# Products without use beside a sink attention, and half of its normalising moved to ScalarE

## The chip, the cores and the metric

The kernel runs on one core of one Trainium2 chip. The metric is the device time of a whole execution in microseconds (us). A core has a matrix engine (TensorE, PE), a vector engine (VectorE, DVE), an engine for activation functions (ScalarE, ACT), GpSimd (POOL) and SyncE (SP), whose queue here issues all transfers (DMA). The engines run side by side, each through its own list in order, and wait for each other by semaphores.

## The reference

Three layers follow each other. The first is an attention with a window and sinks (2 sequences, 8 heads, 768 positions, 64 values per head), the second and third are feed-forward layers on 1536 tokens with a model width of 512 and an inner width of 2048.

```python
def _attn_ref(q, k, v, n_sink, window):          # n_sink = 4, window = 128
    scores = scale * np.matmul(q, k.transpose(0, 1, 3, 2))
    keep = is_sink | in_window                   # pos_k < n_sink, or 0 <= pos_q - pos_k < window
    scores = np.where(keep, scores, -1e9)
    a = np.exp(scores - np.max(scores, axis=-1, keepdims=True))
    a = a / (np.sum(a, axis=-1, keepdims=True) + 1e-09)
    return np.matmul(a, v)

def _moe_ref(x, w_in, w_out):
    h = x @ w_in
    g = np.where(h >= 1, h, np.where(h <= -1, 0.0, (h + 1) ** 2 / 4))
    return g @ w_out

def _moe2_ref(x, w_in, w_out):
    h = x @ w_in
    return (h * np.clip(h + 3.0, 0.0, 6.0) / 6.0) @ w_out
```

The weights come as 8-byte floats, and the kernel narrows them on the chip.

## The kernel before

The attention is cut into units of 128 queries of a pair of heads. A unit goes through several steps. `score` multiplies queries and keys of both heads (L322) into two PSUM banks; DVE adds the mask and finds the extreme of each row (L329); ACT takes the exponential and its sum (`expo`, L348); `normalise` adds a small constant, takes the reciprocal (L340, L341) and multiplies each of the two heads by it (L343). Three units later `turn` transposes the probabilities on PE (L385, L386) and copies them out of PSUM (L367); `sinks` does it for the few sink columns (L397). When all units of a pair are turned, `mix` multiplies them with the values (L422) and splits the result into a high and a low part (L143, L150).

The feed-forward runs in fp32r, each f32 operand split into a high and a low part and three products for one: `h_group` (L546) makes the inner activations of 128 inner columns, two engines apply the activation function and split it (L555 to L560, L143, L150), and `y_group` (L590) adds its share of the output two slots later. The 1536 tokens are taken in chunks of 512, 256, 256 and 512 for the first layer and 512 three times for the second. Weights are loaded (`load_w`, L173), narrowed by DVE and ACT (`narrow`, L185 to L197) and split (`high`, `low`).

Orders: PE and SP keep the order in which the program is written. A list `steps` holds the attention's steps in order; its first 47 (begin, 21 scores, 17 turns, 4 sinks, 4 mixes) run ahead of the feed-forward, one after the other, with the weights taken between them; later steps are spread over the slots of the feed-forward. DVE and ACT are ordered by the compiler's scheduler. A planner (`Balance`) keeps a sum of expected nanoseconds for ACT and DVE; where either engine can do a copy, `pick` gives it to the one with the smaller sum. `defer` puts a piece of work some steps later. PSUM holds two banks for scores (tag "a"), four for outputs of the feed-forward (tags "y0" to "y3", lent to the transposes before) and two for inner activations (tag "h").

Of the kernel before, what the change touches and what calls it, by code (L numbers as in the profile page):

```python
# [8 lines left out]
F32 = mybir.dt.float32  # L9
# [3 lines left out]
AF = mybir.ActivationFunctionType  # L13
# [3 lines left out]
P = 128  # L17
# [8 lines left out]
N = 512  # L26
# [10 lines left out]

AHEAD = 8
WO_LEAD = 2

SLACK = 6

# [33 lines left out]
def sink_attention_moe_moe_kernel(  # L76
# [14 lines left out]
    nc = tc.nc  # L91
    B, H, _, S = q.shape
# [10 lines left out]
    consts = ctx.enter_context(tc.tile_pool(name="consts", bufs=1))  # L103
# [7 lines left out]
    ps_h = ctx.enter_context(tc.tile_pool(name="ps_h", bufs=2, space=bass.MemoryType.PSUM))  # L111
# [11 lines left out]
    def defer(fn, slots=1):  # L123
        waiting.append((clock[0] + slots, fn))

    def tick():
        clock[0] += 1
        due = [w for w in waiting if w[0] <= clock[0]]
        for w in due:
            waiting.remove(w)  # L130
            w[1]()

    def flush():
        while waiting:
            tick()

    bal = Balance()
# [23 lines left out]
        return xparts[ci]  # L161

    half = consts.tile([P, 1], F32, name="half")
    ident = consts.tile([P, P], F32, name="ident")


# [32 lines left out]
    def take(m, which, fc):  # L199

        t = raw.pop((m, which, fc))
        if which == "i":
            hi = wpool.tile([P, DM], F32R, tag=f"wih{fc}", name=f"wih{m}_{fc}")
            lo = wpool.tile([P, DM], F32R, tag=f"wil{fc}", name=f"wil{m}_{fc}")
            wi[m, fc] = (hi.rearrange("p (k f) -> p k f", f=P), lo.rearrange("p (k f) -> p k f", f=P))
        else:
            w = wo_tile(m, fc)
            hi, lo = w[:, 0, :], w[:, 1, :]

        def split(src):  # L210
            high(hi, src, DM)
            defer(lambda: low(lo, src, hi, DM))
            if which == "o":
                defer(lambda: nc.sync.dma_start(out=f32(wo_d[m][fc]), in_=f32(w.rearrange("p a f -> p (a f)"))), 4)

        if wide:
            t32 = raw_p.tile([P, DM], F32, tag="w32", name="w32", bufs=3)
            narrow(t, t32)
            defer(lambda: split(t32), 2)
        else:  # L220
            split(t)
# [27 lines left out]
    def build_fast_attention(at_p):  # L249
        def key_column(i):  # L250
            return i * P + max(i - 1, 0) * NS
# [25 lines left out]
        def geom(gi):  # L277
            ci, b, i0, nq = GROUPS[gi]
            first = max(i0 - 1, 0)
            return b, i0, nq, first, i0 + nq - first  # L280

        def load(j):

            if j >= len(pairs):
                return
            gi, hp = pairs[j]
            b, i0, nq, first, nb = geom(gi)
            k0, k1 = key_column(first), key_column(i0 + nq - 1) + P
            r0 = 2 * hp * P + D
            tq = at_p.tile([P, NQ * P], F32, tag="qraw", name="qraw")[:, :nq * P]  # L290
            nc.sync.dma_start(out=tq, in_=q[b].rearrange("h r s -> (h r) s")[r0:r0 + P, i0 * P:(i0 + nq) * P])
            tk = at_p.tile([P, KW], F32, tag="kraw", name="kraw")[:, :k1 - k0]
            nc.sync.dma_start(out=tk, in_=k[b].rearrange("h r s -> (h r) s")[r0:r0 + P, k0:k1])
            qk[j] = (tq, tk)
# [17 lines left out]
        def score(j, u):  # L312
            b, i0, nq, first, nb = geom(pairs[j][0])
            tq, tk = qk[j]
            i = i0 + u
            w = widths[min(i, 2)]
            c0 = key_column(max(i - 1, 0)) - key_column(first)
            banks = []
            for e in range(2):
                rows = slice(e * D, (e + 1) * D)  # L320
                banks.append(ps_a.tile([P, 512], F32, tag="a", name="ps_s")[:, :w])
                nc.tensor.matmul(  # L322
                    banks[e], tq[rows, u * P:(u + 1) * P], tk[rows, c0:c0 + w], start=True, stop=True
                )
            p = at_p.tile([P, 2, KB + P], F32, tag="p", name="p", bufs=DIST + 3)[:, :, :w]
            nm = at_p.tile([P, 2], F32, tag="nm", name="nm", bufs=DIST + 2)
            sm = at_p.tile([P, 2], F32, tag="sm", name="sm", bufs=DIST + 2)
            for e in range(2):
                nc.vector.tensor_tensor_reduce(  # L329
                    out=p[:, e, :], in0=banks[e], in1=masks[min(i, 2)], scale=-SCALE, scalar=BIG,  # L330
                    op0=ALU.add, op1=ALU.min, accum_out=nm[:, e:e + 1],
                )
                bal.add("dve", 230 + w / 0.96)
            probs[j, u] = p
            if u == nq - 1:
                qk.pop(j)
                load(j + 2)

            def normalise():
                nc.vector.tensor_scalar_add(out=sm, in0=sm, scalar1=1e-9)  # L340
                nc.vector.reciprocal(out=sm, in_=sm)  # L341
                for e in range(2):
                    nc.vector.tensor_scalar_mul(out=p[:, e, :], in0=p[:, e, :], scalar1=sm[:, e:e + 1])  # L343
                bal.add("dve", 300 + 2 * (140 + w / 1.92))

            def expo():
                for e in range(2):
                    nc.scalar.activation(  # L348
                        out=p[:, e, :], in_=p[:, e, :], func=AF.Exp, scale=-1.0, bias=nm[:, e:e + 1],
                        accum_out=sm[:, e:e + 1],  # L350
                    )
                bal.add("act", 2 * (480 + w / 1.2))
                defer(normalise)

            defer(expo)
# [109 lines left out]
    def attend(upto):  # L465
        tick()
        first = True
        while done[0] < min(upto, len(steps)):
            if not first:
                tick()  # L470
            first = False
            steps[done[0]]()
            done[0] += 1
# [150 lines left out]
    def take_weights(s):  # L624
        while taken[0] < len(queue) and queue[taken[0]][0] <= s:
            take(*queue[taken[0]][1:])
            taken[0] += 1
            defer(load_weights, 4)

    x1_d = []  # L630
    with tc.manual_schedule(engines={mybir.EngineType.PE, mybir.EngineType.SP}):
        nc.vector.memset(half, 0.5)
        make_identity(nc, ident)
        with ExitStack() as att:
            if fast:
                at_p = att.enter_context(tc.tile_pool(name="at", bufs=2))
                build_fast_attention(at_p)
                attend(1)
                load_weights()
                n0 = ready[0]  # L640
                while done[0] < n0:
                    attend(done[0] + 1)
                    take_weights(-AHEAD + (AHEAD * done[0]) // n0 - 1)
            else:
                x1_d.append(dram.tile([DM, NT], F32, name="x1_d"))
                dense_attention(x1_d[0])
                load_weights()
                load_x1(0)
            take_weights(-1)
            flush()  # L650

            for s in range(len(seq) + LAG):
                lo = hi = fc = 0
                if s < len(seq):
                    ci, fc = seq[s]
                    m = chunks[ci][0]
                    if fast and ci + 1 < NCH:
                        lo, hi = ready[ci], ready[ci + 1]
                    if fc == 0:
                        flush()  # L660
                    if fc == 4 and ci + 1 < len(chunks):
                        if chunks[ci + 1][0]:
                            load_x(ci + 1)
                        elif not fast:
                            load_x1(ci + 1)
                sub = [0]

                def slot(fc=fc, lo=lo, hi=hi, sub=sub):
                    sub[0] += 1
                    total = 4 * FC - SLACK  # L670
                    attend(lo + (hi - lo) * min(4 * fc + sub[0], total) // total)

                a = s - LAG + WO_LEAD
                if 0 <= a < len(seq) and seq[a][0] not in (0, NCH):
                    load_wo(chunks[seq[a][0]][0], seq[a][1])
                if s < len(seq):
                    h_group(s, slot)
                    take_weights(s)
                    slot()
                if s >= LAG:  # L680
                    y_group(s - LAG, slot)
                slot()
            flush()
# [40 lines left out]
```

## Time and profile before

| | |
|---|---|
| time before, median of 3 runs | 681.76 us (679.98 to 683.12) |
| the profiled execution's own time | 683.12 us |
| its span, first to last instruction | 681.3 us |
| PE busy | 657.6 us (97%) |
| DVE busy | 415.9 us (61%) |
| ACT busy | 336.4 us (49%) |
| mean granted PE clock | 0.977 |

Busy time is the union of an engine's instructions. The granted clock is a share of full speed, 1.00 for 2.4 GHz and 0.50 for 1.2 GHz. PEld is the loading of weights into PE, which can overlap products. A wait is put down to what ended it.

### The profile page before, as it was taken

What the parts mean: (1) busy time and instruction counts of PE and PEld (TensorE: products, weight loads), DVE (VectorE), ACT (ScalarE), POOL (GpSimd) and SP (SyncE); (2) the same over time, 40 slices, a digit from 0 to 9 for tenths busy, and PEclk for the clock granted to TensorE, in tenths of its full rate; (3) what the DMA queues carried; (4) which work ended last, traced back from release to release, by engine and by line L of the source; (5) the groups of instructions that cost most, each with busy time, mean ns of one, the idle gap of its engine ahead of it and who ended that gap; (6) DMA issues with size and microseconds to landing.
All of it is one profiled execution on the core that took longest, in us unless ns stands there. A gap on an engine that the chain in (4) does not pass through costs nothing.

```text
span 681.3 us, 9471 instructions
## 1 busy us (share of the span) xinstructions
PE 657.6 (97%) x3392; PEld 523.7 (77%) x3392; DVE 415.9 (61%) x1031; ACT 336.4 (49%) x711; POOL 3.4 (0%) x19
## 2 busy tenths in 40 slices
PE   6988799999999999999999999999999999999997
PEld 3544567777788998888888887888888888888886
DVE  5978899998765556653779898598332222222222
ACT  5758776775454545553457575475222222322222
POOL 1000000000000000000000000000000000000000
PEclk9957899999999999999999999999999999999999
DMA  7234568656576446252398542994228222153321
GB/s 256 87 86 139 190 197 267 193 180 219 194 287 234 141 170 236 99 181 91 109 400 295 207 159 102 373 377 168 99 81 313 94 93 93 47 202 101 110 68 63
DMA packets 47023, 119.20 MB, mean 175 GB/s; under 512 B 4432, under 2 KB 15744, under 8 KB 46976
## 3 DMA queue, kind: packets, MB, share of 16 engines
q1 hardware_dynamic: 46976, 118.60, 49.9%
q8 instruction: 27, 0.44, 0.3%
q14 instruction: 20, 0.16, 0.1%
HBM read 92.36 MB, written 26.21 MB: 174 GB/s over the span
## 4 chain that ended last, share of the span: by engine, by line
PE 74%; DVE 11%; DMA 9%; ACT 3%; issue 1%; SPq 1%; ACTq 0%
PE ps_y L590 32%; PE ps_h L546 31%; DMA raw0i<-moe_w_in_dram 4%; PE ps_s L322 4%; PE ps_v L422 4%; DVE w L192 2%; DMA raw0o<-moe_w_out_dram 2%; DVE w L197 2%; DMA raw1o<-moe_w_out_dram 1%; PE ps_t L386 1%; DMA raw1i<-moe_w_in_dram 1%; PE ps_t L385 1%; ACT w L187 1%; PE ps_k L397 1%; DVE p L329 1%
## 5 line engine op out<-in xcount | busy, mean ns | idle before, releaser
L590 PE MATMUL ps_y<-gh,wo 128*128 128x512 f32 (+1 forms) x896 | 268.3, 364 | 1.6 <-ACT pt L367 1.3
L590 PEld LDWEIGHTS ps_y<-gh,wo 128*128 128x128 f32 x896 | 163.1, 189 | 31.5 <-issue 4.4
L546 PE MATMUL ps_h<-xh,wih 128*128 128x512 f32 (+1 forms) x448 | 165.9, 370 | 6.1 <-DVE gl L150 5.9
L546 PE MATMUL ps_h<-xl,wih 128*128 128x512 f32 (+1 forms) x448 | 161.5, 360 | 0.0
L546 PE MATMUL ps_h<-xh,wil 128*128 128x512 f32 (+1 forms) x448 | 161.5, 360 | 0.0
L590 PE MATMUL ps_y<-gl,wo 128*128 128x512 f32 (+1 forms) x448 | 160.9, 359 | 0.0
L150 DVE TENSOR_TENSOR gl<-ps_h,gh 128x512 fp32r<-128x512 f32 (+1 forms) x112 | 68.7, 613 | 87.4 <-ACT gh L143 87.3
L143 ACT ACTIVATE gh<-ps_h 128x512 fp32r<-128x512 f32 (+1 forms) x112 | 59.9, 535 | 110.4 <-PE ps_y L590 89.3
L546 PEld LDWEIGHTS ps_h<-xh,wih 128*128 128x128 f32 x448 | 84.7, 189 | 26.0 <-DVE gl L150 8.0
L546 PEld LDWEIGHTS ps_h<-xh,wil 128*128 128x128 f32 x448 | 84.8, 189 | 12.9
L546 PEld LDWEIGHTS ps_h<-xl,wih 128*128 128x128 f32 x448 | 84.9, 190 | 11.8
L590 PEld LDWEIGHTS ps_y<-gl,wo 128*128 128x128 f32 x448 | 84.6, 189 | 12.0
L560 DVE SCALAR_TENSOR_TENSOR ps_h<-r,ps_h 128x512 f32<-128x512 f32 x48 | 33.4, 696 | 85.3 <-ACT r L559 85.3
L559 ACT ACTIVATE r<-ps_h,half 128x512 f32<-128x512 f32 x48 | 33.0, 688 | 89.3 <-PE ps_h L546 89.3
L322 PE MATMUL ps_s<-kraw,qraw 64*128 64x260 f32 (+2 forms) x192 | 50.0, 495 | 11.4 <-DVE nm L329 6.9
L348 ACT ACTIVATE p<-p,nm 128x260 f32<-128x260 f32 (+2 forms) x96 | 46.5, 485 | 26.6 <-DVE nm L329 25.9
L329 DVE CUSTOM_DVE_ANT_0 p<-ps_s,mask 128x260 f32<-128x260 f32 (+2 forms) x96 | 36.8, 401 | 20.0 <-PE ps_s L322 19.8
L322 PEld LDWEIGHTS ps_s<-kraw,qraw 64*128 64x128 f32 x192 | 24.3, 228 | 27.9 <-DVE nm L329 14.8
L555 ACT ACTIVATE r<-ps_h,half 128x512 f32<-128x512 f32 (+1 forms) x64 | 36.7, 573 | 17.6 <-PE ps_h L546 17.1
L556 DVE SCALAR_TENSOR_TENSOR r<-r 128x512 f32<-128x512 f32 (+1 forms) x64 | 35.4, 554 | 15.5 <-ACT r L555 15.4
L190 DVE TENSOR_SCALAR w<-w 128x512 f32<-128x512 f32 x64 | 27.0, 422 | 17.1 <-ACT w L187 16.9
L557 DVE TENSOR_TENSOR ps_h<-ps_h,r 128x512 f32<-128x512 f32 (+1 forms) x64 | 35.9, 562 | 0.8
(59 smaller groups left out, 587.9 us busy)
## 6 DMA issues: line engine op xcount, KB each, us to landing
wo<-wo_d SPq DMA_DIRECT2D x80, 512.0 KB, 4.0
wo_d<-wo SPq DMA_DIRECT2D x32, 512.0 KB, 5.5
raw0i<-moe_w_in_dram SPq DMA_DIRECT2D x16, 512.0 KB, 4.7
raw0o<-moe_w_out_dram SPq DMA_DIRECT2D x16, 512.0 KB, 5.1
raw1i<-moe_w_in_dram SPq DMA_DIRECT2D x16, 512.0 KB, 5.4
raw1o<-moe_w_out_dram SPq DMA_DIRECT2D x16, 512.0 KB, 5.2
xh<-x2h_d SPq DMA_DIRECT2D x3, 1024.0 KB
xl<-x2l_d SPq DMA_DIRECT2D x3, 1024.0 KB, 9.5
```

The source lines that it names most:

```text
L143: nc.scalar.activation(out=dst, in_=src, func=AF.Copy)
L150: nc.vector.tensor_tensor(out=dst, in0=src, in1=f32(hi), op=ALU.subtract)
L322: nc.tensor.matmul(banks[e], tq[rows, u * P:(u + 1) * P], tk[rows, c0:c0 + w], start=True, stop=True)
L329: nc.vector.tensor_tensor_reduce(out=p[:, e, :], in0=banks[e], in1=masks[min(i, 2)], scale=-SCALE, scalar=BIG, op0=ALU.add, op1=ALU.min, a ...
L348: nc.scalar.activation(out=p[:, e, :], in_=p[:, e, :], func=AF.Exp, scale=-1.0, bias=nm[:, e:e + 1], accum_out=sm[:, e:e + 1],)
L546: nc.tensor.matmul(ps, w[:, kc, :], x[:, kc, :], start=i == 0, stop=i == len(ops) - 1)
L555: nc.scalar.activation(out=r, in_=ps, func=AF.Relu, scale=0.5, bias=half)
L556: nc.vector.scalar_tensor_tensor(out=r, in0=r, scalar=1.0, in1=r, op0=ALU.min, op1=ALU.mult)
L557: nc.vector.tensor_tensor(out=ps, in0=ps, in1=r, op=ALU.max)
L559: nc.scalar.activation(out=r, in_=ps, func=AF.Relu, scale=1.0 / 6.0, bias=half)
L560: nc.vector.scalar_tensor_tensor(out=ps, in0=r, scalar=1.0, in1=ps, op0=ALU.min, op1=ALU.mult)
L590: nc.tensor.matmul(ys[dm], a[:, cs], b, start=fc == 0 and i == 0, stop=fc == FC - 1 and i == 2)
```

## The change

`normalise` multiplies the first head on DVE as before; the second head is multiplied by ACT, as a copy with a scale per row, and the planner is told of it. A constant tile `warm` of 128x128 is filled with 0.5 by DVE. Ahead of the first chunk's feed-forward, eight products of `warm` with itself are issued on PE before the first score, and one after each of the following attention steps. They go to a tile of one of the two "h" banks, which nobody reads.

```diff
+WARM = 8
+WARM_STEP = 1
...
+    warm = consts.tile([P, P], F32, name="warm")
...
             def normalise():
                 nc.vector.tensor_scalar_add(out=sm, in0=sm, scalar1=1e-9)
                 nc.vector.reciprocal(out=sm, in_=sm)
-                for e in range(2):
-                    nc.vector.tensor_scalar_mul(out=p[:, e, :], in0=p[:, e, :], scalar1=sm[:, e:e + 1])
-                bal.add("dve", 300 + 2 * (140 + w / 1.92))
+                nc.vector.tensor_scalar_mul(out=p[:, 0, :], in0=p[:, 0, :], scalar1=sm[:, 0:1])
+                nc.scalar.activation(out=p[:, 1, :], in_=p[:, 1, :], func=AF.Copy, scale=sm[:, 1:2])
+                bal.add("dve", 300 + 140 + w / 1.92)
+                bal.add("act", 190 + w / 1.2)
...
+    def keep_warm(ps, n):
+        for _ in range(n):
+            nc.tensor.matmul(ps, warm, warm, start=True, stop=True)
+
...
+        nc.vector.memset(warm, 0.5)
         nc.vector.memset(half, 0.5)
...
                 attend(1)
                 load_weights()
                 n0 = ready[0]
+                idle = ps_h.tile([P, N], F32, tag="h", name="idle")[:, :P]
+                keep_warm(idle, WARM)
                 while done[0] < n0:
                     attend(done[0] + 1)
+                    keep_warm(idle, WARM_STEP)
                     take_weights(-AHEAD + (AHEAD * done[0]) // n0 - 1)
```

## Rows read from the trace of the kernel before

**Rows 1.** Windows around the first feed-forward product: length, busy us (instructions) per engine, clock, DMA.
```profile
0.00:74.07 74.07, 62.26 (x241) 33.68 (x241) 56.41 (x221) 52.20 (x141) 3.38 (x19) 0.82 0.43 142
74.07:120.00 45.93, 39.81 (x187) 29.26 (x186) 42.27 (x98) 30.91 (x63) 0.00 (x0) 0.96 0.70 231
120.00:681.30 561.30, 555.59 (x2969) 460.72 (x2967) 317.27 (x714) 253.24 (x508) 0.00 (x0) 1.00 0.50 175
```

**Rows 2.** Chain that ended last, 0 to 120 us: start us, us, what.
```profile
44.24 4.23 PE ps_v L422 x20
...
70.03 4.14 PE ps_v L422 x20
...
75.09 4.08 DMA raw0i<-moe_w_in_dram
```

**Rows 3.** Windows cut at changes of the granted clock: PE, PEld, DVE, ACT, POOL, clock.
```profile
4.00:36.30 32.30, 27.16 (x88) 14.70 (x88) 26.73 (x103) 22.75 (x62) 0.00 (x0) 1.00 0.53 177
36.30:50.00 13.70, 13.14 (x48) 7.22 (x50) 9.42 (x40) 8.47 (x25) 0.00 (x0) 0.50 0.14 48
50.00:56.80 6.80, 6.21 (x40) 3.46 (x38) 5.62 (x27) 5.99 (x18) 0.00 (x0) 1.00 0.74 235
56.80:60.20 3.40, 3.40 (x20) 2.03 (x18) 3.40 (x11) 3.40 (x11) 0.00 (x0) 0.50 0.02 6
60.20:63.60 3.40, 1.89 (x11) 0.91 (x10) 3.40 (x12) 2.10 (x6) 0.00 (x0) 1.00 0.66 199
63.60:73.90 10.30, 10.30 (x42) 5.36 (x42) 7.60 (x32) 8.21 (x22) 0.00 (x0) 0.50 0.36 120
```

**Rows 4.** Timeline of PE: start us, us, line, form, count, idle time before.
```profile
22.30 0.42 PE L386 MATMUL ps_t<-ident,p 128*128 128x128 f32 x1
22.51 0.42 PE L385 MATMUL ps_t<-ident,p 128*128 128x128 f32 x1
...
36.73 2.18 PE L322 MATMUL ps_s<-kraw,qraw 64*128 64x260 f32 x4 [2.08 <-DVE nm L329]
...
39.31 0.42 PE L385 MATMUL ps_t<-ident,p 128*128 128x128 f32 x1
39.53 0.42 PE L386 MATMUL ps_t<-ident,p 128*128 128x128 f32 x1
...
50.60 0.27 PE L385 MATMUL ps_t<-ident,p 128*128 128x128 f32 x1
50.72 0.27 PE L386 MATMUL ps_t<-ident,p 128*128 128x128 f32 x1
...
52.92 0.71 PE L322 MATMUL ps_s<-kraw,qraw 64*128 64x260 f32 x4
53.56 0.44 PE L386 MATMUL ps_t<-ident,p 128*128 128x128 f32 x2
...
66.57 1.24 PE L322 MATMUL ps_s<-kraw,qraw 64*128 64x260 f32 x4
67.74 0.47 PE L385 MATMUL ps_t<-ident,p 128*128 128x128 f32 x1
```

**Rows 5.** Groups by line and form, DVE and ACT, 0 to 74 us: busy us, mean ns.
```profile
L343 DVE TENSOR_SCALAR p<-p,sm 128x260 f32<-128x260 f32 x24 | 7.4, 351 | 0.0
...
L348 ACT ACTIVATE p<-p,nm 128x260 f32<-128x260 f32 x26 | 13.0, 501 | 1.0 <-DVE nm L329 1.0
...
L367 ACT ACTIVATE pt<-ps_t 128x512 f32<-128x512 f32 x13 | 7.6, 583 | 1.5 <-PE ps_t L386 1.3
```

**Rows 6.** Timeline, the first work on ACT and on PE.
```profile
0.73 1.28 ACT L348 ACT_TABLE_LOAD   x1 [0.73 <-PEq L717]
...
4.30 0.80 PE L322 MATMUL ps_s<-kraw,qraw 64*128 64x128 f32 x4 [4.30 <-DMA kraw<-k_dram]
```

**Rows 7.** Timeline of PE behind the first feed-forward group.
```profile
84.45 0.79 PE L546 MATMUL ps_h<-xh,wih 128*128 128x512 f32 x1 [3.67 <-DVE gl L150]
```

## What is predicted

> **What bounds the kernel now.** I read the windows first, cut where TensorE (PE) starts the first feed-forward product, at 74.07 us [rows 1]. From 120 us to the end PE is busy for 555.6 of 561.3 us at a clock of 1.00: nothing can be bought there, since both edits leave those products as they are. From 74 to 120 us PE idles 6.1 of 45.9 us while VectorE (DVE) is busy for 42.3. Before 74 us no engine is full: PE 62.3, DVE 56.4, ScalarE (ACT) 52.2 of 74.07. So the price of the change is decided ahead of 74 us, and what it wins there must then pass the stretch up to 120 us. Whatever PE is ahead by then stays won, because from there on PE is full.
>
> Second, the chain of waits: much of the stretch before 74 us is PE itself, in runs of scores, transposes and above all mixes [rows 2]. Third, the windows cut where the granted clock changes [rows 3]. The column reads 0.50 (1.2 GHz) from 36.3 to 50.0, 56.8 to 60.2 and 63.6 to 73.9 us, together 27.4 us in which PE is busy almost throughout, and 1.00 (2.4 GHz) between. It rose at the end of runs of mix products, as of those that begin at 44.24 and 70.03 us [rows 2], and fell after waits, as at 36.3 us inside a wait of 2.08 us [rows 4].
>
> Ahead of 36.3 us the column reads 1.00, but I don't believe it for all of that: the reader is to compare the starts of neighbouring transposes [rows 4]. At 22 us they lie 0.21 us apart, as at 39 us where the column says 0.50 (0.22); at 50.6 us, where it says 1.00, 0.12. So PE was at half rate at 22 us too, and I take that for most of the time up to there. The Trainium skill says the same of the state that the array starts in ("TensorE: Matmul & The Clock Gate", Part 1): throttled, until activity releases it; the spacing at 22 us agrees with it and not with the column.
>
> Is PE's half rate what costs time, or do DVE and ACT set the pace? Window by window [rows 3]: from 4 to 36.3 us DVE is busy for 26.7 of 32.3 and from 50.0 to 63.6 us for 12.4 of 13.6: there DVE leads. From 36.3 to 50.0 it is busy for 9.4 of 13.7 and from 63.6 to 73.9 us for 7.6 of 10.3, ACT for 8.5 and 8.2, and PE for 13.1 and 10.3: there PE at 1.2 GHz leads. These two stretches are what a faster clock can shorten.
>
> **The products without use.** A step adds one product of 128x128 by 128x128 in f32. The trace has none of just that form; a score, also f32, shows four MATMUL instructions for its two heads [rows 4], so a product is two, and each streams 128 columns as a transpose does: 0.21 us at the lower and 0.11 us at the upper level. One product is 0.42 or 0.22 us. The first eight cost 8 x 0.42 = 3.4 us. They need only a memset; engines start at 0.73 us, and the first score waits for its keys until 4.30 us [rows 6]. From about 1.0 the products end at about 4.4: hidden but for 0.1 to 0.2 us. If their weight loads did not overlap, they would take up to twice that, 3 us on the path; the transposes, each with its own weight load, follow each other without such a gap, so I take the low end.
>
> The list of steps up to the first chunk's last mix has 47 entries (begin, 21 scores, 17 turns, 4 sinks, 4 mixes), so 46 products follow: 9 of them in the first PE-led stretch and 7 in the second, by the order of scores, turns and mixes in the trace. On the chain about 11.8 us of the first (its 13.7 less 1.9 us of waiting for DVE) and all 10.3 of the second are PE at the lower level: 22.1 us. At the upper level a score takes 0.64 us to the next start in place of 1.17, and a transpose about half [rows 4]; so 22.1 becomes 11.1 and saves 11.0. The 16 products cost 16 x 0.22 = 3.5. Net 7.5 us, if the clock is up throughout. Bounds: clock up and all products inside waits, 11.0 gained; clock down throughout, 16 x 0.42 = 6.7 lost. I take 7.5, near the upper bound, because the products use all rows and columns of the array, as the mixes do, and stand where PE now waits behind a score. They read a constant and write a bank that nobody reads: they wait for nobody, and only the next step on PE waits for them. The bank is one of the two that the feed-forward uses after them.
>
> **Half of the normalising on ACT.** DVE's multiplication of one head takes 351 ns; the nearest ACT row is the exponential on the same tile, also with a per-partition operand, 501 ns [rows 5]. The exponential also sums up; a plain copy of 512 columns is 583 ns, which by width alone would make 260 columns 0.30. Between the two I take 0.41. Before 74 us 40 such multiplications run on DVE (24 of the form shown, 16 narrower), so 20 move: DVE loses 20 x 0.31 (less than a row's 0.35, since neighbours overlap) = 6 us, ACT gains 8. In the whole kernel 48 move; behind 120 us PE's full row covers them. No function table has to be loaded again: copies and exponentials already share one load of 1.28 us [rows 6].
>
> But the planner is told too. It gives each copy and split to the engine with the smaller sum. In its own prices DVE has for the stage 20 x 1.85 + 8.5 weights x 2.2 = 56 us, ACT 20 x 1.4 + 8.5 x 0.6 + 24 of evictions and splits = 57, with the evictions of transposes on ACT [rows 5]. With the move ACT would be 13 ahead, so some 5 to 6 us of evictions and splits go the other way. DVE gets only about 1 us lighter, ACT about 3 heavier. I credit 0.5 us for the stretches that DVE leads, and not the 3 that half of the 6 would be.
>
> The Trainium skill has a rule against this half ("ScalarE: Activation LUTs", Rules for kernel authors): multiplications belong on VectorE, not ScalarE. By the rows the single instruction is indeed dearer, 0.41 to 0.50 against 0.31 to 0.35; by that rule this half would lose 20 x 0.1 = 2 us and gain nothing, and the sum would be 2.5 us worse. That ACT becomes too full is the second rival.
>
> **Sum.** 7.5 + 0.5 - 0.2 = 7.8 us earlier at the first feed-forward product. What of it survives to 120 us? There the chain runs through loads of raw weights, ACT and DVE; such a load is on it at 75.09 us, issued by SyncE in order behind what waits for the last mix [rows 2], so it comes earlier with PE. PE stands 3.67 us for one split of an activation, which is ACT's and DVE's work [rows 7]. DVE's work per microsecond stays as it is (42.3 of 45.9), so most of the gain moves through; ACT, fuller by some 3 us and holding the very split for which PE stands, takes part of it. I take a quarter as lost: 6 us. Against the profiled run's own 683.1 us (span 681.3 and 1.8 around it) that is 677.1. This run lies 1.4 us above the median of 681.76, so I forecast 675.5 us.
>
> **Rivals.** (1) *The clock does not stay up, and it ends slower.* Place: 4 to 74 us. The 46 products then cost 0.42 each, 19.3 us; PE's waits of the stage (74.07 - 62.3 - 4.3 = 7.5 us) hide some. Price: between 6.7 (the PE-led stretches alone) and 19.3 - 7.5 = 11.8, so 688 to 694. It decides when less than half of the 22 us on the chain runs at 2.4 GHz: with a share f there the gain is 11.0 f - 3.5 f - 6.7 (1 - f), zero at f = 0.47. For it: the lower level held from 36.3 to 50.0 us although PE was busy for 13.1 of them. Against: what filled that stretch at first was scores of 64 rows and transposes, and the full-array mixes at its end raised the clock. Chance 0.16.
> (2) *The gain is given back.* PE arrives earlier and then waits for weights or for a split on ACT, which at 52 + 8 us (if the planner shifts little) is the fullest engine of a stage of 66. For it: the wait of 3.67 us ended by such a split. Against: all idle time of PE in these 46 us is now 6.1. Nothing to 3 us is left: 679 to 682. Chance 0.22; the edge of it counts as faster.
> (3) *The relief of DVE counts whole.* The planner shifts little and ACT still fits: 2.5 us more than credited, nothing lost after 74 us, and 5 further units times 0.31 = 1.6 there: 7.8 + 2.5 + 1.6 = 11.9, or 670. Chance 0.12.
>
> **Numbers.** What a measurement of this kernel can tell from no change is about 0.5%, 3.4 us. The forecast, 671 to 679 us, has 0.50. Faster: 0.50 + 0.12 + 0.03 of rival 2; same 0.19; slower 0.16. The range leaves out most of rival 1 and a rest below: 666 to 684.
>
> **What would show it.** The clock column at 1.00 and transposes 0.11 to 0.12 us apart from about 5 to 8 us on; the first feed-forward product at about 66 us; 108 new MATMULs of 128x128, most at the upper level; ACT multiplications at 0.41 to 0.50 us, half of DVE's gone, and some evictions on DVE; the feed-forward from 120 us on unchanged in length. Wrong if the clock falls between mixes as now, or if the first feed-forward product comes early and PE's idle time in the next 46 us grows by as much.

## The result, and the profile after

The change makes the kernel slower: 685.33 us, median of 20 runs (682.22 to 687.02), against 681.52 for the kernel before in the same comparison. The ratio estimated from the executions timed in turn is 1.0067, with a 95% interval of 1.0049 to 1.0084 (the quotient of the two medians is 1.0056). One of before's 20 executions, at 730.51 us, fell in a slow state and is left out of the ratio. The forecast was 675.5 us. The profiled execution after took 682.83 us, among the lowest of its 20 runs, while the one shown of before took 683.12, well above its median; so the two traces may be compared for where time lies, and not for how much the change costs.

First the windows after, cut at the first and at the third feed-forward group (the columns are those of [rows 1]) and at the first group of the second chunk:

```profile
0.00:71.06 71.06, 61.84 (x348) 42.48 (x349) 53.47 (x206) 54.00 (x150) 3.40 (x19) 0.88 0.45 148
71.06:85.70 14.64, 7.23 (x34) 4.98 (x33) 12.69 (x27) 12.02 (x23) 0.00 (x0) 0.93 0.67 229
85.70:185.20 99.50, 97.48 (x470) 72.62 (x471) 86.25 (x204) 67.37 (x141) 0.00 (x0) 0.98 0.61 197
185.20:681.00 495.80, 491.51 (x2651) 411.81 (x2650) 256.67 (x557) 219.26 (x440) 0.00 (x0) 1.00 0.49 173
```

The first feed-forward product starts 3.0 us earlier than in [rows 1], not 7.8. And the first row holds the main reading of this study: PE is busy for 61.84 us before it, as against 62.26. The attention's own work on PE has become much shorter, and PE is as full as it was. Counted from each instruction's start to the next start on PE, less waits, the attention takes 40.7 us where it took 62.3, and the products take 21.1, of which 3.7 lie ahead of the first score. PE's waits behind its first product are 8.2 us in all, where they were 7.5 behind the first score.

Then the groups before 71 us that the change made or moved (columns as in [rows 5]):

```profile
L637 PE MATMUL idle<-warm 128*128 128x128 f32 x107 | 25.9, 343 | 1.1 <-DVE half L642 1.1
...
L347 ACT ACTIVATE p<-p,sm 128x260 f32<-128x260 f32 x11 | 5.5, 498 | 1.0 <-DVE sm L345 1.0
L346 DVE TENSOR_SCALAR p<-p,sm 128x260 f32<-128x260 f32 x12 | 4.3, 354 | 0.2
...
L374 DVE COPY pt<-ps_t 128x512 f32<-128x512 f32 x3 | 2.1, 686 | 0.2
...
L189 DVE TENSOR_SCALAR w<-raw0i 128x512 int32<-128x512 int32 x3 | 1.3, 426 | 3.3 <-DMA raw0i<-moe_w_in_dram 3.3
```

The products cover 25.9 us, more than the 21.1 above, since the end of one product overlaps what follows it. The planner answers the move in the way that was forecast: evictions (L374) and a step of the narrowing (L189) now also run on DVE, which is 2.9 us lighter in this stage, with ACT 1.8 us heavier.

The clock, by windows cut where it changes:

```profile
12.10:18.90 6.80, 6.80 (x26) 5.07 (x26) 6.17 (x24) 6.59 (x19) 0.00 (x0) 0.50 0.53 198
...
29.20:32.60 3.40, 3.40 (x18) 1.72 (x16) 3.40 (x12) 2.71 (x8) 0.00 (x0) 0.50 0.00 0
...
42.80:49.70 6.90, 6.90 (x32) 4.23 (x32) 2.72 (x13) 3.57 (x13) 0.00 (x0) 0.51 0.16 50
49.70:71.06 21.36, 20.54 (x145) 13.87 (x145) 18.57 (x71) 18.76 (x55) 0.00 (x0) 1.00 0.51 159
```

And PE's timeline, start and length in us:

```profile
1.05 3.78 PE L637 MATMUL idle<-warm 128*128 128x128 f32 x16 [1.05 <-DVE half L642]
...
5.41 0.49 PE L637 MATMUL idle<-warm 128*128 128x128 f32 x2
...
14.26 0.64 PE L637 MATMUL idle<-warm 128*128 128x128 f32 x2
...
15.98 0.80 PE L637 MATMUL idle<-warm 128*128 128x128 f32 x2
16.57 0.42 PE L390 MATMUL ps_t<-ident,p 128*128 128x128 f32 x1
...
21.31 0.27 PE L391 MATMUL ps_t<-ident,p 128*128 128x128 f32 x1
21.42 0.27 PE L390 MATMUL ps_t<-ident,p 128*128 128x128 f32 x1
...
51.98 0.49 PE L637 MATMUL idle<-warm 128*128 128x128 f32 x2
52.31 0.27 PE L390 MATMUL ps_t<-ident,p 128*128 128x128 f32 x1
...
85.72 0.79 PE L551 MATMUL ps_h<-xh,wih 128*128 128x512 f32 x1 [6.56 <-DVE gl L153]
```

In this execution the half rate ends with the eight products: a product takes 0.49 us at 5.41 us and 0.64 at 14.26, where the column reads 0.50, and at 21 us transposes lie 0.11 us apart where they lay 0.21 apart [rows 4]. The clock still falls three times, for 17.1 us in all, as against 27.4 recorded us [rows 3] and the unrecorded ones ahead of them. These reach from the first score at 4.30 to the first run of mixes, as PE's timeline of before shows: at 22 us its transposes lay 0.21 us apart, and behind the mixes 0.11:

```profile
29.49 3.25 PE L422 MATMUL ps_v<-pt,vraw 128*64 128x256 f32 x16
...
32.94 0.27 PE L386 MATMUL ps_t<-ident,p 128*128 128x128 f32 x1
33.05 0.27 PE L385 MATMUL ps_t<-ident,p 128*128 128x128 f32 x1
```

The timeline after also gives the price of one product, from its start to the next start on PE: 0.33 us at 51.98 with the clock up, 0.59 at 15.98 with the clock down. Behind the steps it is mostly 0.32 to 0.42 and 0.56 to 0.59, not the 0.22 and 0.42 that two transposes would take.

Last, the wait behind the first feed-forward groups: 3.67 us became 6.56 [rows 7]. ACT, DVE and SyncE in that place:

```profile
71.83 0.34 SPq L177 DMA_DIRECT2D raw0i<-moe_w_in_dram  x1
...
76.13 0.66 ACT L191 ACTIVATE w<-raw0i 128x512 f32<-128x512 f32 x1 [1.79 <-DMA raw0i<-moe_w_in_dram]
...
77.77 0.68 ACT L560 ACTIVATE r<-ps_h,half 128x512 f32<-128x512 f32 x1
...
83.20 0.57 ACT L146 ACTIVATE gh<-ps_h 128x512 fp32r<-128x512 f32 x1
...
84.98 0.68 DVE L153 TENSOR_TENSOR gl<-ps_h,gh 128x512 fp32r<-128x512 f32 x1
```

ACT's list has the narrowing of a weight ahead of the first activation (L560). The weight was asked for at 71.83 and ACT stood for it until 76.13. In the kernel before the first activation stands ahead of that narrowing:

```profile
77.17 0.69 ACT L555 ACTIVATE r<-ps_h,half 128x512 f32<-128x512 f32 x1 [2.38 <-PE ps_h L546]
79.26 0.67 ACT L187 ACTIVATE w<-raw0i 128x512 f32<-128x512 f32 x1 [1.41 <-DMA raw0i<-moe_w_in_dram]
```

So the first activation started 3.1 us after the first product before and starts 6.7 us after it now. Nobody wrote this order: DVE and ACT are ordered by the compiler's scheduler, and in every kernel here that was left to it, after any edit, the two lists came out in another order than before.

### The profile page after: what moved, and what is told of

The parts are those of the page before. It is cut to its first block, busy times and chain, and to the rows that moved or that the text cites. A ratio compares the mean times of both kernels' runs of the same rounds, so it can differ in the third digit from the quotient of the medians.

```text
span 681.0 us, 9710 instructions
## 1 busy us (share of the span) xinstructions
PE 658.1 (97%) x3500; PEld 531.9 (78%) x3500; DVE 409.1 (60%) x991; ACT 352.7 (52%) x752; POOL 3.4 (0%) x19
## 4 chain that ended last, share of the span: by engine, by line
PE 82%; DVE 10%; DMA 5%; ACT 1%; issue 1%; SPq 1%; ACTq 0%
PE ps_h L551 35%; PE ps_y L595 35%; PE ps_v L427 4%; PE ps_s L326 3%; DMA raw0i<-moe_w_in_dram 3%; DVE w L201 2%; DVE w L196 2%; DMA raw0o<-moe_w_out_dram 1%; PE ps_t L391 1%; PE idle L637 1%; DVE w L194 1%; DVE wil L153 1%; PE ps_t L390 1%; DVE p L333 1%; DMA raw1o<-moe_w_out_dram 1%
## 5 line engine op out<-in xcount | busy, mean ns | idle before, releaser
L326 PE MATMUL ps_s<-kraw,qraw 64*128 64x260 f32 (+2 forms) x192 | 39.6, 434 | 6.6 <-DVE nm L333 6.5
L560 ACT ACTIVATE r<-ps_h,half 128x512 f32<-128x512 f32 (+1 forms) x64 | 36.7, 573 | 15.3 <-PE ps_h L551 14.6
L326 PEld LDWEIGHTS ps_s<-kraw,qraw 64*128 64x128 f32 x192 | 18.7, 196 | 17.8 <-DVE nm L333 9.3
```

The source lines that it names most:

```text
L326: nc.tensor.matmul(banks[e], tq[rows, u * P:(u + 1) * P], tk[rows, c0:c0 + w], start=True, stop=True)
L560: nc.scalar.activation(out=r, in_=ps, func=AF.Relu, scale=0.5, bias=half)
```

## The experiments

Ratios are to the kernel before, timed in turn on the same chip. "First group" is the start of the first feed-forward product and "to third" the time from there to the first product of the third group, each in the one profiled execution.

| run | ratio (95% interval) | first group, us | to third, us |
|---|---|---|---|
| the change | 1.0067 (1.0049 to 1.0084) | 71.1 | 14.7 |
| products alone | 1.0067 (1.0029 to 1.0105) | 71.7 | 14.5 |
| move alone, planner told | 1.0050 (1.0018 to 1.0082) | 63.9 | 14.6 |
| eight products alone | 1.0008 (0.9977 to 1.0038) | 71.4 | 10.7 |
| move alone, planner not told | 1.0012 (0.9984 to 1.0041) | 69.1 | 12.0 |
| products, old order | 1.0023 (0.9995 to 1.0050) | 72.2 | 10.3 |
| no products, their order | 1.0033 (1.0005 to 1.0061) | 69.4 | 15.7 |
| both, old order | 1.0039 (1.0010 to 1.0067) | 68.2 | 10.6 |
| move, old order | 1.0003 (0.9971 to 1.0035) | 73.5 | 10.4 |
| products of four rows, old order | 1.0415 (1.0375 to 1.0454) | 98.9 | 10.8 |
| half of the products, old order | 1.0020 (0.9989 to 1.0051) | 71.5 | 9.5 |
| twice the products, old order | 1.0047 (1.0016 to 1.0077) | 73.3 | 9.5 |
| the change, activation first | 1.0022 (0.9996 to 1.0049) | 70.6 | 8.9 |
| early products, old order | 0.9977 (0.9948 to 1.0006) | 70.9 | 10.1 |
| late products, old order | 1.0026 (1.0000 to 1.0053) | 73.0 | 9.5 |

**The halves.** Products alone:

```diff
-                nc.vector.tensor_scalar_mul(out=p[:, 0, :], ...)
-                nc.scalar.activation(out=p[:, 1, :], ..., scale=sm[:, 1:2])
+                for e in range(2):
+                    nc.vector.tensor_scalar_mul(out=p[:, e, :], ...)
```

> The kernel before with the products without use alone; both heads stay on VectorE. Theory A (the products lengthen the kernel: they reorder ACT and DVE at the start of the feed-forward, or hold PE): ratio 1.004 to 1.008, most of the whole change's 1.0067. Theory B (the move to ScalarE is what costs): ratio 0.99 to 1.001, and the first feed-forward product at 66 to 71 us.

The move alone leaves out `keep_warm` and the tile `warm`:

> The kernel before with the second head moved to ScalarE alone, the planner told, no products. Theory A: ratio 0.997 to 1.002. Theory B: 1.004 or more, with PE waiting longer than 6 us behind the first feed-forward groups for splits that come late on ACT.

Eight products alone have `WARM_STEP = 0` beside the edit of the first:

> Only the first eight products, none behind the steps, both heads on VectorE. If the products per step keep the clock up, the clock here falls soon after the first scores as before, and the first feed-forward product stays at 73 to 75 us; time ratio 0.997 to 1.003. If the eight by themselves delay the start, about 1.001 to 1.003.

And the move alone with the planner's old sums:

```diff
-                bal.add("dve", 300 + 140 + w / 1.92)
-                bal.add("act", 190 + w / 1.2)
+                bal.add("dve", 300 + 2 * (140 + w / 1.92))
```

> The move to ScalarE alone, but the planner keeps its old sums. If the planner's shifting of evictions back to VectorE is what loses the relief, this is faster than the told move by 1 to 3 us; if ScalarE is then too full, slower by as much, with ACT some 4 us busier and DVE some 4 us less busy before the feed-forward.

Both halves lose by themselves, 1.0067 and 1.0050, so neither A nor B was whole. Their losses don't add up to the change's, which points to a cause that they share. It shows in the last column: those that lose most need 14.5 us or more from the first to the third group, and the two that don't lose measurably need 10.7 and 12.0. With the eight products alone the first group started at 71.4 us, not at 73 to 75 as expected. With the planner not told the move was 2.6 us faster than with it told (1.0012 against 1.0050), as the first of the two expectations had it; the intervals overlap.

**The order, held.** Four kernels have the lists of DVE and ACT pinned, by edges of mere order from each instruction to the next, to those of another kernel. `ORDER` holds that kernel's places (the edit is shortened here, and the moved multiplications are left free where there are any):

```diff
+        for name, engine in (("DVE", ...), ("ACT", ...)):
+            want = [mine[int(n)] for n in ORDER[name].split()]
+            for a, b in zip(want, want[1:]):
+                tc.add_manual_dep(b, a.name, NoSync, reason="order")
```

Products alone, in the order of the kernel before:

> The products alone, with the instruction lists of ACT and DVE held in the order that they have in the kernel before. Theory O (the products win time by the clock, but the compiler's scheduler answers them with another order on ACT and DVE, in which the first feed-forward groups wait for weights): ratio 0.992 to 0.998, and 10 to 11 us from the first to the third feed-forward group as before, not 14.6. Theory P (the products take PE's time, or ACT and DVE are too full to give the clock's gain back in any order): 1.003 to 1.008 as with the products alone in their own order.

The kernel before, in the order of the products alone:

> No products and no move; the kernel before, with the lists of ACT and DVE in the order that the scheduler made for the products alone. Theory O: 1.004 to 1.009, 14 us or more from the first to the third feed-forward group. Theory P: 0.998 to 1.002.

Both halves, planner not told, in the old order, and the move likewise:

> Products and move, the planner not told of the move, everything else on ACT and DVE in the order of the kernel before (the moved multiplications find their own places). Theory O: 0.985 to 0.996, the best of all. Theory P: 1.000 to 1.008.

> The move alone, planner not told, everything else in the order of the kernel before. Theory O: 0.994 to 1.001, below the 1.0012 of the untold move in its own order. If ScalarE is the bound: 1.002 or more.

The crossing is plain in the last column: with the old order 10.3 to 10.6 us in all three kernels, as before (10.4), with the new one and no product at all 15.7. In the time the order by itself is worth 0.33% (0.05 to 0.61), short of the 0.4 to 0.9 that theory O expected. Where products stand beside it, the difference is 0.44% (1.0067 - 1.0023); from the two intervals its own error is estimated at 0.47, so this pair alone would not show it. The kernel before in the new order, on ACT and on PE:

```profile
74.65 0.67 ACT L249 ACTIVATE w<-raw0i 128x512 f32<-128x512 f32 x1 [0.97 <-DMA raw0i<-moe_w_in_dram]
...
76.56 0.69 ACT L617 ACTIVATE r<-ps_h,half 128x512 f32<-128x512 f32 x1
```

```profile
69.43 0.50 PE L608 MATMUL ps_h<-xh,wih 128*128 128x512 f32 x1
...
85.12 0.80 PE L608 MATMUL ps_h<-xh,wih 128*128 128x512 f32 x1 [2.82 <-DVE gl L212]
```

The place is the same: the narrowing of an input weight stands ahead of the first activation in all four kernels of the table with 14.5 us or more, where that activation starts 6.6 to 7.6 us after the first product, and in none of the others, where it starts after 3.0 to 5.0 us.

But theory O expected more: with the old order the products should have won. They didn't (1.0023, not told from 1), nor with the move (1.0039). So a second cause stood open: what the products cost on PE.

**What a product costs and wins.** All in the old order. Products of the same columns that use 4 rows of the array:

```diff
-            nc.tensor.matmul(ps, warm, warm, start=True, stop=True)
+            nc.tensor.matmul(ps, warm[0:4, :], warm[0:4, :], start=True, stop=True)
```

> As the products alone in the old order, but each product uses 4 rows of the constant tile and not 128: the same columns and the same instructions on PE. Theory C (each product costs PE's time on the path, and a higher clock pays most of it back): the clock is as low as in the kernel before, and the time is 5 to 12 us above it (1.007 to 1.018). Theory H (products hide in PE's waits, and the clock wins nothing, because ACT and DVE set the pace): 0.999 to 1.004 as with all rows.

Half and twice as many behind the steps (`WARM_STEP * (done[0] % 2)`, `WARM_STEP = 2`):

> As the products alone in the old order, with a product behind every second step (23 in place of 46). Theory C: 4 to 5 us less PE time, of which a lower clock takes some back: 0.995 to 1.000. Theory H: 1.001 to 1.003, nothing changes.

> As the products alone in the old order, with two products behind each step (92). Theory C: 46 further products of 0.22 us with the clock already up, 6 to 10 us more than the single ones: 1.010 to 1.017. Theory H: 1.001 to 1.005.

And the kernel before once more, for a second profile (682.27 us):

> The kernel before once more, for a second profile: another placing of the stretches at the lower clock, and with it a first feed-forward product between 66 and 73 us. If the times of its executions differ by the clock alone, the stretch from the 17th feed-forward group to the end lasts 496 us as in the first profile.

The four-row products cost 28 us. The windows of that kernel up to its first feed-forward product, its product group, and PE's timeline:

```profile
0.00:98.90 98.90, 97.85 (x349) 58.18 (x349) 57.26 (x224) 54.27 (x142) 3.40 (x19) 1.00 0.32 107
```

```profile
L698 PE MATMUL idle<-warm 4*128 4x128 f32 x108 | 40.1, 486 | 1.1 <-DVE half L703 1.1
```

```profile
40.60 0.42 PE L451 MATMUL ps_t<-ident,p 128*128 128x128 f32 x1
40.81 0.42 PE L452 MATMUL ps_t<-ident,p 128*128 128x128 f32 x1
41.16 0.79 PE L698 MATMUL idle<-warm 4*128 4x128 f32 x2
41.88 1.24 PE L388 MATMUL ps_s<-kraw,qraw 64*128 64x260 f32 x4
```

PE is busy for 97.85 of 98.90 us, and transposes lie 0.21 us apart: the half rate, although the column reads 1.00. So here the products are wholly on the path, and the upper clock does not come before the feed-forward. With all rows it comes: the same count of instructions, 26.7 us less until the first group (98.9 against 72.2). The products do not hide in PE's waits here, and in that H fails. But C fails in its number: 1.0415 is far above its 1.007 to 1.018, and the clock is lower than in the kernel before, which first left the half rate at some 33 us. Nor is the difference the clock's alone. A product of four rows takes 0.72 us to the next start (41.16 to 41.88), one of all rows mostly 0.56 to 0.59 at the same rate; over 46 products that makes an estimated 6 to 7 us.

What the clock gives back is about what the products cost. Compare two kernels without products, the kernel before again and the move alone, whose clock stood at the upper level from the middle of the attention on in its profiled execution, the fastest of its 12 (677.82 us, with a median of 683.5):

```profile
0.00:70.90 70.90, 58.12 (x241) 31.68 (x241) 54.38 (x216) 50.30 (x138) 3.41 (x19) 0.88 0.44 148
```

```profile
0.00:63.94 63.94, 50.72 (x241) 28.22 (x241) 51.30 (x200) 51.07 (x144) 3.40 (x19) 1.00 0.50 164
```

PE is busy for 50.7 us there, and the first group starts at 63.9. That is at most the prize of a high clock if nothing is paid for it, since DVE is lighter there too (51.3 against 54.4 us). Twice the products reach nearly that clock (0.98 in the stage), and start the first group at 73.3; half of them, at 71.5. From start to start, less waits, half, single and twice the products take 13.6, 21.9 and 30.3 us of PE before the first group, and the attention 47.8, 41.3 and 36.5: each step of the count wins on the attention most of what it costs, and PE waits less (9.0, 7.9 and 5.4 us). The mean recorded clock over all executions rises alike, 0.976, 0.981 and 0.991.

The times of both runs lie where H expected them (half 1.0020 in 1.001 to 1.003, twice 1.0047 in 1.001 to 1.005). C's 1.010 to 1.017 for twice the products is excluded by the interval; its 0.995 to 1.000 for half of them is not. So neither theory holds whole: the products are paid on PE, as C has it, and the count hardly matters, as H has it.

The second profile of the kernel before met its expectation for the first group (70.9 us), but its stretch from the 17th group to the end lasts 497.6 us and not 496: executions of one kernel differ by a microsecond there too, and not only by the clock ahead of the feed-forward.

**Which place of the order, and which products.** In the changed kernel, the place in ACT's list put right, by an edge of mere order; `first` collects the activations of the groups:

```diff
+            if which == "i" and 0 < len(first) <= 4:
+                with tc.issue_after(first[-1]):
+                    narrow(t, t32)
+            else:
+                narrow(t, t32)
```

> The changed kernel whole, with one edit: the narrowing of the four input weights that are taken behind the first four feed-forward groups must stand behind the activation of its group in ACT's list. Theory O1 (of the new order, it is this one place that costs: the first activation stands behind a weight that has not landed): 10 to 11 us from the first to the third feed-forward group in place of 14.6, and 2 to 3 us of the 4.5 lost are won back: 1.002 to 1.004. Theory O2 (the loss of the order is spread over the list): 1.005 to 1.008.

```profile
73.63 0.69 ACT L566 ACTIVATE r<-ps_h,half 128x512 f32<-128x512 f32 x1 [1.61 <-PE ps_h L557]
74.21 0.66 ACT L191 ACTIVATE w<-raw0i 128x512 f32<-128x512 f32 x1
...
78.70 0.69 DVE L153 TENSOR_TENSOR gl<-ps_h,gh 128x512 fp32r<-128x512 f32 x1
```

The first activation now waits for PE alone, the third group starts 8.9 us after the first, and two thirds of the loss are gone (1.0067 to 1.0022). The time is in the range of O1, and the third group comes even sooner than its 10 to 11 us. But the edit did more than move one place: the scheduler made both lists anew, and they differ from the change's in dozens of places. Of the 5.8 us won to the third group, 3.6 lie ahead of the first activation, and 1.4 of these are earlier splits of the attention's output; the other 2.1 lie behind it. So the loss of the order sits around the first groups; that this one place makes all of it is not shown.

Products only up to the 24th step, and only behind it (then without the eight):

```diff
-                    keep_warm(idle, WARM_STEP)
+                    keep_warm(idle, WARM_STEP * (done[0] <= 24))
```

> The products alone in the old order, but only up to the 24th step, in the stretch that DVE leads; none behind it. Theory C (each product is paid on PE, and the clock pays it back about even): 0.998 to 1.002, with the clock falling after some 45 us as before. If the early products hide behind DVE and leave the clock up for the rest: 0.992 to 0.997, faster than both kernels.

> The complement of the early products, in the old order: none before the first score and none up to the 24th step, one behind each of the steps after it (23). Theory C1 (products are paid where PE leads and hide where VectorE leads): 1.001 to 1.005, slower than the early ones by 2 us or more. Theory C2 (a product costs and wins the same wherever it stands): 0.996 to 1.000, as the early ones.

Windows of the early, the late, and no products (before again), up to 24 us and from there to the first group:

```profile
0.00:24.00 24.00, 22.95 (x83) 17.11 (x84) 16.02 (x65) 15.78 (x43) 3.38 (x19) 1.00 0.60 198
24.00:70.90 46.90, 38.63 (x222) 23.58 (x219) 38.59 (x152) 34.87 (x96) 0.00 (x0) 0.85 0.37 123
```

```profile
0.00:24.00 24.00, 17.50 (x47) 9.62 (x48) 16.47 (x69) 16.21 (x44) 3.38 (x19) 1.00 0.58 198
24.00:73.00 49.00, 44.26 (x240) 27.61 (x240) 38.68 (x152) 34.76 (x97) 0.00 (x0) 0.86 0.37 118
```

```profile
0.00:24.00 24.00, 17.48 (x47) 9.55 (x48) 16.29 (x66) 16.89 (x45) 3.41 (x19) 1.00 0.57 198
24.00:70.90 46.90, 40.64 (x195) 22.13 (x194) 38.09 (x151) 33.41 (x95) 0.00 (x0) 0.82 0.38 123
```

Early products fill time in which PE stood (22.95 against 17.5 us of 24) and delay nobody: the first long run of mixes starts at 29.3 us, as against 29.2 without products. But they bought little clock in this execution: its transposes lie 0.21 us apart until 23 us, although the column reads 1.00. Late ones make PE 3.6 us busier behind 24 us and the stretch 2.1 us longer, with the clock scarcely higher. Late ones are 3.3 us slower than early ones (1.0026 against 0.9977), as theory C1 expected. The early ones come out best of all kernels here, 0.9977, between the two expectations, but the interval holds 1: they beat the changed kernel, and that they beat the one before is not shown.

## Why the prediction was wrong, by its steps

**What bounds the stage: right, with one gap.** In the stretches that PE leads its half rate does set the pace, and that the clock's column says nothing of the level before its first change was right too: the four-row products read 1.00 for 99 us at half rate. What I missed is where the shown execution stands among the others. Over 35 executions of the kernel before, timed beside the held orders, the time falls by 0.39 us for each thousandth of recorded mean clock (least squares, 0.975 to 0.992; a microsecond at the lower level costs about 0.29). The profiled one, at 0.977, has its first group at 74.1 us, the second profile, at 0.984, at 70.9. By this pair a typical execution has some 3 us less to win ahead of the feed-forward; the forecast took 1.4 off for it.

**Sixteen products at 3.5 us: the term that failed in size.** The prediction charged 16 of 46 products at 0.22 us and let the other 30 hide in PE's waits. Neither holds. A product takes 0.33 to 0.42 us with the clock up and 0.56 to 0.59 with it down, and the 46 together take 17.4 us of PE in the changed kernel. PE's waits did not shrink for them (8.2 us, 7.5 before): a product stands behind a step by the list, not in a wait, and only the ones up to the 24th step are seen to delay nobody. PE's saving was larger than the 11.0 us counted, as the half rate of the first 33 us ended early too: the attention takes 17 us less (second profile of before against the products in the old order) or 22 us less (the two profiles of [rows 1] and of the change). The products took about as much. The clock was not up throughout, but fell three times. The reason given for that, that the mixes use all rows and columns as the products do, misread them: they use 128 rows and 64 columns (128*64 in their rows). In place of 7.5 us won, the products in the old order came out at 1.0023 of the time, 1.6 us lost (by the interval -0.3 to 3.4). The eight products ahead delay the first score by 0.46 us (4.76 in place of 4.30), where 0.1 to 0.2 were forecast.

The first rival's 19.3 us for 46 products is close to the 17.4 by luck: it took 0.42 us each at the lower level, where 0.56 to 0.59 were measured, and the clock was mostly at the upper. Its condition was too narrow: with a clock that is up for two thirds of the stage the balance is still not positive.

**What survives to 120 us: the step that failed in kind.** The prediction held DVE's and ACT's lists to be as they were and took off a quarter for a fuller ACT. The second rival had the place (the split behind which PE stands) and half of the mechanism: it is not how full ACT is, but what stands ahead of the activation in its list. The 3.0 us won by the first group were lost by the third, which comes 4.3 us later after the first than it did. In the 46 us behind the first product PE idles for 8.1 us in place of 6.1; the prediction had named such a growth as a sign of being wrong. Beyond the 17th group both kernels run alike: 495.8 us to the end after and 496.2 before. The order makes 0.33 to 0.45% of the 0.67 (the kernel before in the new order, and the change with its activation first). The rest is not told apart between the products, the move and nothing.

**The move to ScalarE: right as to cost, and not told from harmless.** The multiplication takes 498 ns, at the upper bound of 0.41 to 0.50, and the planner's answer was of the kind forecast. In the old order the move measures 1.0003 (0.9971 to 1.0035); told to the planner, in the order that then results, 1.0050. The rule of the Trainium skill ("ScalarE: Activation LUTs", Rules for kernel authors) agrees with the single instruction, 498 against 354 ns; the 2 us that the prediction drew from it are neither seen in the time nor excluded by the interval. The told move's order is worse than the untold one's (14.6 and 12.0 us to the third group) in the same place: the narrowing stands ahead of the first activation, which starts 7.6 us after the first product, and 4.5 in the untold one.

## What to carry to other kernels

Work that only keeps a clock up has to stand where the engine would otherwise be idle; on its path it has to earn more than it costs, and here the two were even within the noise. Take its price from the start of one such piece to the next start among the work that it will stand in: between other steps a product took half as much again as two transposes in a row. Before reading a change's profit off a trace, ask which lists a scheduler will order anew: hold the order and time the change again, and time the new order without the change. And where executions differ by the clock, take two profiles of the kernel before ahead of any sum.

## What the runs showed that was not expected

Products of the same columns and count, once with 128 rows and once with 4, made 26.7 us of difference until the first feed-forward group, most of it by the clock: with 4 rows PE did not leave its half rate before the feed-forward. With 128 rows it left it at some 5 us in the changed kernel, but in the profiles of the early products and of half the products only at 24 to 27 us, so the eight products ahead do not settle it. And two instruction lists, with no other change to the program, were worth 5 us between the first and the third feed-forward group.
